# Linear-attention denominators: per-feature products moved to VectorE, one mask matmul per chunk, and the steps around them reordered

## Chip, cores and metric

The kernel runs on one core of one Trainium2 chip. The metric is device time in microseconds, the median of several executions. The profile describes one execution; its span (first to last instruction) is about 2 us shorter than the device time. PE is TensorE (PEld its weight loads), DVE is VectorE, ACT ScalarE, POOL GpSimd. "Granted clock" is the share of full TensorE speed that the chip allowed.

## The reference, cut to what matters

```python
xn = layernorm(x)                                  # x: 1 x 2048 x 640, bf16
q, k, v = split(xn @ wqkv)                         # 32 heads of 20 features
phi = lambda t: where(t > 0, t + 1, exp(t)) + 1e-6
pq, pk = phi(q), phi(k)
kv  = einsum("bhsd,bhse->bhde", pk, v);  z = einsum("bhsd->bhd", pk)
num = einsum("bhqd,bhde->bhqe", pq, kv)
den = einsum("bhqd,bhd->bhq", pq, z)[..., None] + 1e-6     # <- the change is about this
out = x + (num / den).reshape(...) @ wo + (gelu(xn @ w1 + b1) @ w2 + b2)
```

## The kernel before

Tokens stand in 16 tiles of 128 and in 4 chunks of 512. The 640 query features lie in five column groups j of 128 partitions (4 features of each of 32 heads in a group). The stages in PE's order: transposes and the GELU layer; keys for all tiles; the key-value product; query chunk 0; z; the key-value transform; query chunk 1; the product M with the output weights; chunk 0's denominator; query chunks 2 and 3; then 16 output tiles, each of 24 matmuls for the GELU branch and 10 for attention, accumulated in PSUM. In the timelines below each engine runs its instructions in the order in which the program lists them, so that order decides what waits for what. The parts that matter:

```python
def phi(src, b, nb, dst, res_dst, extra_w):        # after each query group
    scalar: et = Exp(src)
    vector: et = min(et, 1) + 1e-6
    vector: dst = max(src, 0) + et                 # src in PSUM
...
def z_step():                                      # z_sb[p, j]: sum of phi(k)
    ...
    for j in range(DT):                            # z on the head mask, one matrix per group
        vector: ZB[:, j, :] = bmask * z_sb[:, j:j+1]
...
def den_step(c):                                   # one chunk of 512 tokens
    for j in range(5): tensor: bank += ZB[:, j, :].T @ PQ[:, j, cc]
    vector: den_sb = bank + 1e-6
    vector: rden = reciprocal(den_sb)
    for j in range(5): vector: PQ[:, j, cc] *= rden
...
q_chunk(0); z_step(); kvt_step(); q_chunk(1); m_step(); den_step(0); q_chunk(2); q_chunk(3)
for c in range(4): x_again(c)                      # DMA x again, over xnT: after its last reader
for t in range(16): xb(t)                          # gpsimd: x_res[t] += b2
for t in range(16):
    out_tile(t)                                    # ends with vector: out = PSUM + x_res[t]
    if t % 4 == 0 and t // 4 + 1 < 4: den_step(t // 4 + 1)
```

Code is shortened here: `vector:` stands for an instruction recorded on that engine.

## Time and profile before

| | before |
|---|---|
| device time | 223.33 us, median of four runs (223.21, 223.23 and 223.43 fast; 255.02 slow) |
| PE busy | 214.4 of 221.4 us (97%) |
| VectorE / GpSimd busy | 125.8 / 41.7 us |
| granted clock | 1.00 |

From the page of the kernel before: busy time of an engine, its share, its number of instructions; then the busy share in 40 slices of the span, in tenths, and the granted clock.

```profile
span 221.4 us, 3944 instructions
PE 214.4 (97%) x1603; PEld 148.6 (67%) x1612; DVE 125.8 (57%) x227; ACT 74.3 (34%) x140; POOL 41.7 (19%) x74
...
PE   7699999999999999999999999999999999999994
...
DVE  2767778500004888899078549889929414811211
...
POOL 2246554200000000000000000079993000000000
PEclk9999999999999999999999999999999999999999
```

PE is the limit: every slice but the ramp (the start-up) and the last is full. VectorE has room, and GpSimd's second busy stretch (slices 27 to 31) is the 16 bias additions.

From the chain of waits of the kernel before (start us, duration us, engine, tile, line), around chunk 0's denominator; L504 is its matmuls, L507, L509 and L511 its eviction, reciprocal and multiplies, L548 the output tiles.

```profile
129.19 1.04 PE ps L504 x4
...
130.26 0.70 DVE den_sb L507
...
130.98 3.36 DVE rden L509
...
134.37 1.77 DVE PQ L511 x5
...
141.27 4.78 PE ps L548 x34
```

Two things are to be read here. Five denominator matmuls take 1.08 us where a group is recorded whole (0.215 us each; here one record is missing). And the normalization takes VectorE 5.88 us (130.26 to 136.14) while PE works on query chunks 2 and 3: the chain passes through VectorE, but PE loses only 0.26 us, just before 141.27.

From the timeline of the kernel before (start, duration, engine, line, operation, count): the multiplies of chunk 0, those of chunk 1, a residual addition between, and GpSimd's additions.

```profile
134.37 1.77 DVE L511 TENSOR_TENSOR PQ<-PQ,rden 128x512 bf16<-128x512 bf16 x5
...
146.85 0.82 DVE L554 TENSOR_TENSOR out_sb<-ps,xnT 128x640 bf16<-128x640 f32 x1 [0.74 <-POOL xnT L520]
...
151.69 6.88 DVE L511 TENSOR_TENSOR PQ<-PQ,rden 128x512 bf16<-128x512 bf16 x5
...
145.35 22.60 POOL L520 TENSOR_TENSOR xnT<-xnT,b2bc 128x640 bf16<-128x640 bf16 x16 [102.12 <-DMA xnT<-in_A_x_dram]
```

The same five multiplies take 1.77 us alone and 6.88 us beside GpSimd. Chunk 1's columns are ready at 158.57 us and first needed in tile 4, whose attention part starts at 164.08 us.

### The profile page before, as it was taken

To read this page: it belongs to the slowest core of one execution; us is meant where nothing else is said; L and a number is where in the kernel's file an instruction comes from. 1 tells how busy PE (TensorE), PEld (TensorE's weight loads), DVE (VectorE), ACT (ScalarE), POOL (GpSimd) and SP (SyncE) were. 2 spreads that over 40 slices of the span, in tenths; PEclk is the share of its full clock that TensorE was granted. 3 is DMA by queue.
4 is the path that set the end of the run, shared out by engine and by line. 5 is a ranking of instruction groups with operands and counts; after the bars stand their busy time and mean duration, and the time that the engine had idled before them with its cause. 6 is when DMAs were issued, how large, how long until landed. Compare 5 with 4: busy or idle time off the path is not lost.

```text
span 221.4 us, 3944 instructions
## 1 busy us (share of the span) xinstructions
PE 214.4 (97%) x1603; PEld 148.6 (67%) x1612; DVE 125.8 (57%) x227; ACT 74.3 (34%) x140; POOL 41.7 (19%) x74
## 2 busy tenths in 40 slices
PE   7699999999999999999999999999999999999994
PEld 2489999544447777777665865567767776777773
DVE  2767778500004888899078549889929414811211
ACT  2378877566667555111254542600000000000000
POOL 2246554200000000000000000079993000000000
PEclk9999999999999999999999999999999999999999
DMA  5999960000000000000000000254520010010011
GB/s 156 340 363 364 362 233 0 1 3 0 0 0 0 3 0 3 0 0 3 0 0 1 3 0 0 66 173 119 170 70 30 30 60 32 0 62 30 30 46 47
DMA packets 13706, 15.50 MB, mean 70 GB/s; under 512 B 632, under 2 KB 13688, under 8 KB 13688
## 3 DMA queue, kind: packets, MB, share of 16 engines
q1 hardware_dynamic: 13688, 15.24, 21.1%
q8 instruction: 13, 0.21, 0.4%
q14 instruction: 5, 0.04, 0.1%
HBM read 12.62 MB, written 2.62 MB: 69 GB/s over the span
## 4 chain that ended last, share of the span: by engine, by line
PE 88%; DVE 5%; DMA 3%; SPq 1%; issue 1%; DVEq 0%
PE ps L548 33%; PE ps L350 23%; PE ps L438 10%; PE ps L427 10%; PE ps L460 5%; PE ps L494 3%; DMA xPK<-in_A_x_dram 3%; PE ps L504 2%; PE ps L334 2%; DVE PQ L417 2%; DVE rden L509 2%; DVE PQ L511 1%; SPq L235 1%; PE ps L480 1%; SPq L231 1%
## 5 line engine op out<-in xcount | busy, mean ns | idle before, releaser
L350 PE MATMUL ps<-xnT,W 128*128 128x128 bf16 (+2 forms) x447 | 54.8, 279 | 2.1 <-DVE xnT L342 1.9
L548 PE MATMUL ps<-W,HG 128*128 128x320 bf16 x384 | 54.9, 299 | 0.3 <-DVE PQ L417 0.3
L548 PEld LDWEIGHTS ps<-W,HG 128*128 128x128 bf16 x384 | 37.5, 98 | 15.7 <-issue 0.7
L350 PEld LDWEIGHTS ps<-xnT,W 128*128 128x128 bf16 x450 | 36.1, 98 | 17.1 <-DVE xnT L342 1.5
L354 ACT ACTIVATE HG<-ps,b1c 128x128 bf16<-128x128 f32 (+2 forms) x90 | 41.1, 489 | 18.9 <-PE ps L350 17.5
L520 POOL TENSOR_TENSOR xnT<-xnT,b2bc 128x640 bf16<-128x640 bf16 x16 | 22.6, 1448 | 102.1 <-DMA xnT<-in_A_x_dram 102.1
L554 DVE TENSOR_TENSOR out_sb<-ps,xnT 128x640 bf16<-128x640 f32 x15 | 12.3, 823 | 33.4 <-PE ps L548 31.6
L414 ACT ACTIVATE ek<-ps 128x512 bf16<-128x512 f32 (+1 forms) x36 | 23.2, 645 | 23.8 <-PE ps L427 9.2
L415 DVE TENSOR_SCALAR ek<-ek 128x512 bf16<-128x512 bf16 (+1 forms) x36 | 10.9, 304 | 30.7 <-ACT ek L414 29.5
L548 PE MATMUL ps<-Msb,PQ 128*128 128x320 bf16 x160 | 24.5, 299 | 0.0
L427 PE MATMUL ps<-Wqkv,xnT 128*128 128x320 bf16 x160 | 21.9, 299 | 0.0
L438 PE MATMUL ps<-xPK,xn_tm 128*128 128x320 bf16 x160 | 21.9, 299 | 0.0
L460 PE MATMUL ps<-xnT,Wqkv 128*128 128x512 bf16 x97 | 21.6, 379 | 0.2
L427 PEld LDWEIGHTS ps<-Wqkv,xnT 128*128 128x128 bf16 x160 | 15.7, 98 | 6.2
L548 PEld LDWEIGHTS ps<-Msb,PQ 128*128 128x128 bf16 x160 | 15.7, 98 | 6.1
L438 PEld LDWEIGHTS ps<-xPK,xn_tm 128*128 128x128 bf16 x160 | 15.7, 98 | 6.1
L460 PEld LDWEIGHTS ps<-xnT,Wqkv 128*128 128x128 bf16 x100 | 11.7, 117 | 9.5
L307 DVE BATCH_NORM_STATS2 stats<-xPK 128x6 f32<-128x320 bf16 x32 | 15.1, 471 | 4.4 <-DMA xPK<-in_A_x_dram 4.4
L417 DVE SCALAR_TENSOR_TENSOR PQ<-ps,ek 128x512 bf16<-128x512 f32 x20 | 13.8, 692 | 2.1
L417 DVE SCALAR_TENSOR_TENSOR xPK<-ps,ek 128x640 bf16<-128x640 f32 x16 | 13.2, 825 | 1.7
L509 DVE RECIPROCAL rden<-den_sb 128x512 bf16<-128x512 f32 x4 | 13.4, 3353 | 0.1
L511 DVE TENSOR_TENSOR PQ<-PQ,rden 128x512 bf16<-128x512 bf16 x20 | 12.2, 674 | 0.1
(50 smaller groups left out, 113.6 us busy)
## 6 DMA issues: line engine op xcount, KB each, us to landing
xnT<-in_A_x_dram SPq DMA_DIRECT2D x4, 640.0 KB, 4.4
Wqkv<-in_A_wqkv_dram SPq DMA_DIRECT2D x3, 800.0 KB, 12.0
out_dram<-out_sb SPq DMA_DIRECT2D x15, 160.0 KB, 1.8
W<-in_B_w_dram SPq DMA_DIRECT2D x4, 480.0 KB, 5.7
xPK<-in_A_x_dram SPq DMA_DIRECT2D x3, 640.0 KB, 8.6
W<-in_B_w_dram SPq DMA_DIRECT2D x1, 1920.0 KB, 14.2
Wo<-in_A_wo_dram SPq DMA_DIRECT2D x1, 800.0 KB, 10.7
xPK<-in_A_x_dram SPq DMA_DIRECT2D x4, 160.0 KB, 4.8
```

The costliest lines, as they stand in the source:

```text
L307: Pl.ins(v, lambda e: e.bn_stats(stats[:, s, 6 * h:6 * h + 6], x_in[:, t, h * HW:(h + 1) * HW]), reads=[r_x[t]], writes=[r_stats[s]])
L350: Pl.ins("tensor", [(lambda e, k=k: e.matmul(bank(b, 0, w), W1[:, k, jb * P:(jb + 1) * P], xnT[:, k, tok], start=(k == 0), stop=(k == DT - ...
L354: Pl.ins("scalar", lambda e: e.activation(HG[:, jb, tok], bank(b, 0, w), ACT.Gelu_apprx_tanh, bias=b1c[:, jb:jb + 1]), reads=[B_[b], r_b1c ...
L414: Pl.ins("scalar", lambda e: e.activation(e2, src, ACT.Exp), reads=br, writes=[r_ek[s]])
L417: Pl.ins(v, lambda e: e.scalar_tensor_tensor(out=d2, in0=src, scalar=0.0, in1=e2, op0=ALU.max, op1=ALU.add), reads=br + [r_ek[s]], writes= ...
L427: fns.append(lambda e, k=k, h=h, b=b, t=t: e.matmul(bank(b + h, 0, HW), xnT[:, k, t * P:(t + 1) * P], Wqkv[:, k, D + h * HW:D + (h + 1) * ...
L438: Pl.ins("tensor", [(lambda e, t=t, h=h, b=b, f=f: e.matmul(bank(b + h, 0, HW), xn_tm[:, t, f * P:(f + 1) * P], PK[:, t, h * HW:(h + 1) * ...
L460: Pl.ins("tensor", [(lambda e, k=k, j=j, b=b: e.matmul(bank(b), Wqkv[:, k, j:D:DT], xnT[:, k, cc], start=(k == 0), stop=(k == DT - 1))) fo ...
L509: Pl.ins(v, lambda e: e.reciprocal(rden[:], den_sb[:]), reads=[r_den], writes=[r_rden])
L511: Pl.ins(v, lambda e, j=j: e.tensor_tensor(out=PQ[:, j, cc], in0=PQ[:, j, cc], in1=rden[:], op=ALU.mult), reads=[r_rden, r_PQ[c][j]], writ ...
L520: Pl.ins(g, lambda e: e.tensor_tensor(out=x_res[:, t, :], in0=x_res[:, t, :], in1=b2bc[:], op=ALU.add), reads=[r_xr[t // CH], r_b2], write ...
L548: return lambda e: e.matmul(bank(b + h, 0, HW), seq[i][0], seq[i][1][:, h * HW:(h + 1) * HW], start=(i == 0), stop=(i == n - 1))
```

## The change

The intent is to take work off the limiting engine. The sum over the 20 features of a head is a sum over five groups and over four partitions. The old kernel does both in five matmuls. The new one multiplies each group by z and sums the groups on VectorE, and one matmul with the plain head mask sums the partitions. To get the products done ahead of time, the diff also moves steps. Its core, with cuts marked:

```diff
+        q_chunk(0)                       # right after the keys
+        q_chunk(1)
         ... key-value product ...
-            for j in range(DT):          # in z_step
-                Pl.ins(v, lambda e, j=j: e.tensor_scalar(ZB[:, j, :], bmask[:], z_sb[:, j:j + 1], None, ALU.mult), ...)
...
         def den_step(c):
+            Pl.ins(v, lambda e: e.tensor_scalar(den_sb[:], PQ[:, 0, cc], z_sb[:, 0:1], None, ALU.mult), ...)
+            for j in range(1, DT):
+                last = j == DT - 1
+                Pl.ins(v, lambda e, j=j, last=last: e.scalar_tensor_tensor(
+                    out=sden[:] if last else den_sb[:], in0=PQ[:, j, cc], scalar=z_sb[:, j:j + 1],
+                    in1=den_sb[:], op0=ALU.mult, op1=ALU.add), ...)
+
+        def den_step2(c):
-            Pl.ins("tensor", [(lambda e, j=j: e.matmul(bank(b), ZB[:, j, :], PQ[:, j, cc], ...)) for j in range(DT)], ...)
+            Pl.ins("tensor", lambda e: e.matmul(bank(b), bmask[:], sden[:], start=True, stop=True), ...)
             ... eviction, reciprocal, five multiplies as before ...
...
-        q_chunk(0)
         z_step()
         kvt_step()
-        q_chunk(1)
+        q_chunk(2)
+        den_step(0)
         m_step()
-        den_step(0)
-        q_chunk(2)
         q_chunk(3)
+        den_step2(0)
...
         for t in range(NT):
-            out_tile(t)
             if t % CH == 0 and t // CH + 1 < NC:
                 den_step(t // CH + 1)
+            out_tile(t)
+            if t % CH == 1 and t // CH + 1 < NC:
+                den_step2(t // CH + 1)
```

More of the change, by code (lines that the diff above doesn't have):

```diff
@@ L165, in bass_parallel_sum__linear_attn_block__dense_activation_gelu__prompt_kernel @@
         maskKV = [sb(f"maskKV{t}", [P, Wd[t]], BF16) for t in range(DT)]
-        ZB = sb("ZB", [P, DT, P], BF16)
+        sden = sb("sden", [P, CW], BF16)
         onesb = sb("onesb", [P, 1], BF16)
@@ L221, in bass_parallel_sum__linear_attn_block__dense_activation_gelu__prompt_kernel @@
         r_M = [R_("M%d" % j) for j in range(DT)]
-        r_zsum, r_zhl, r_z, r_ZB = R_("zsum"), R_("zhl"), R_("z"), R_("ZB")
+        r_zsum, r_zhl, r_z, r_sden = R_("zsum"), R_("zhl"), R_("z"), R_("sden")
         r_den, r_rden = R_("den"), R_("rden")
@@ L431, in bass_parallel_sum__linear_attn_block__dense_activation_gelu__prompt_kernel, with q_chunk @@
             phi(pair(b), b, 2, PK[:, t, :], r_PK[t], [r_x[t]])
+        def q_chunk(c):
+            cc = slice(c * CW, (c + 1) * CW)
+            for j in range(DT):
+                b = take(1)
+                Pl.ins("tensor", [(lambda e, k=k, j=j, b=b: e.matmul(
+                    bank(b), Wqkv[:, k, j:D:DT], xnT[:, k, cc],
+                    start=(k == 0), stop=(k == DT - 1))) for k in range(DT)],
+                    reads=[r_Wq] + r_xnT[c * CH:(c + 1) * CH], writes=[B_[b]])
+                phi(bank(b), b, 1, PQ[:, j, cc], r_PQ[c][j], [])
+        q_chunk(0)
+        q_chunk(1)
         Pl.ins(v, lambda e: e.memset(KVT, 0.0), writes=[r_KVT] + r_W1)
@@ L453, in bass_parallel_sum__linear_attn_block__dense_activation_gelu__prompt_kernel @@
                reads=[r_zsum, r_zhl], writes=[r_zhl])
-        def q_chunk(c):
-            cc = slice(c * CW, (c + 1) * CW)
-            for j in range(DT):
-                b = take(1)
-                Pl.ins("tensor", [(lambda e, k=k, j=j, b=b: e.matmul(
-                    bank(b), Wqkv[:, k, j:D:DT], xnT[:, k, cc],
-                    start=(k == 0), stop=(k == DT - 1))) for k in range(DT)],
-                    reads=[r_Wq] + r_xnT[c * CH:(c + 1) * CH], writes=[B_[b]])
-                phi(bank(b), b, 1, PQ[:, j, cc], r_PQ[c][j], [])
         def z_step():
@@ L472, in z_step @@
             Pl.ins(v, lambda e: e.tensor_copy(z_sb[:], bank(b, 0, DT)), reads=[B_[b]], writes=[r_z])
-            for j in range(DT):
-                Pl.ins(v, lambda e, j=j: e.tensor_scalar(ZB[:, j, :], bmask[:], z_sb[:, j:j + 1], None, ALU.mult),
-                       reads=[r_z, r_bmask], writes=[r_ZB])
         def kvt_step():
@@ L502, in den_step @@
             cc = slice(c * CW, (c + 1) * CW)
+            Pl.ins(v, lambda e: e.tensor_scalar(den_sb[:], PQ[:, 0, cc], z_sb[:, 0:1], None, ALU.mult),
+                   reads=[r_z, r_PQ[c][0]], writes=[r_den])
+            for j in range(1, DT):
+                last = j == DT - 1
+                Pl.ins(v, lambda e, j=j, last=last: e.scalar_tensor_tensor(
+                    out=sden[:] if last else den_sb[:], in0=PQ[:, j, cc], scalar=z_sb[:, j:j + 1],
+                    in1=den_sb[:], op0=ALU.mult, op1=ALU.add),
+                    reads=[r_z, r_PQ[c][j], r_den], writes=[r_sden if last else r_den])
+        def den_step2(c):
+            cc = slice(c * CW, (c + 1) * CW)
             b = take(1)
-            Pl.ins("tensor", [(lambda e, j=j: e.matmul(bank(b), ZB[:, j, :], PQ[:, j, cc],
-                                                       start=(j == 0), stop=(j == DT - 1))) for j in range(DT)],
-                   reads=[r_ZB] + r_PQ[c], writes=[B_[b]])
+            Pl.ins("tensor", lambda e: e.matmul(bank(b), bmask[:], sden[:], start=True, stop=True),
+                   reads=[r_bmask, r_sden], writes=[B_[b]])
             Pl.ins(v, lambda e: e.tensor_single_scalar(den_sb[:], bank(b), 1e-6, ALU.add),
```

## The prediction

> **What bounds the kernel now.** TensorE. The page's first part has PE busy 97% of a 221.4 us span, and the chain of waits is 88% PE, 5% VectorE. The granted clock is at full speed in every slice. VectorE is busy 57%, GpSimd 19%. In the timeline the only PE gap after the ramp is 0.26 us before the first output tile (141.27 us).
>
> **Removed.** Four of five denominator matmuls per chunk, four chunks: 16. The chain shows such a group of five as 1.08 us, so 0.215 us each: 3.4 us of PE work, on the chain. Five small mask multiplies (1.4 us of VectorE) go too, off the chain.
>
> **Added.** Per chunk one tensor_scalar and four scalar_tensor_tensor of 128x512 on VectorE. The trace has 690 ns for the eviction form and 692 ns for the existing scalar_tensor_tensor of that width; estimate 3.4 us a chunk, 13.7 us in all. VectorE has room in total, so the question is where the work stands.
>
> **Moved.**
> 1. Query chunks 0 and 1 go ahead of the key-value product. The matmul that needs its last eviction (ACT, 0.70 us) is then covered only by the z matmuls (0.36 us): estimate 0.45 us PE wait. The old 0.26 us gap goes.
> 2. Chunk 0's normalization (denominator eviction 0.69, reciprocal 3.35, five multiplies 1.77 us, uncontended) stood between the M product and query chunks 2 and 3, with two chunks of PE work to hide it. Now it follows the last query chunk. Let T be the end of that chunk on PE (estimate 140.4 us). The last phi ends at T+1.7, the reciprocal at T+5.8. Output tile 0 needs the normalized columns at T+3.5 (24 matmuls, 3.26 us, after the one mask matmul).
> 3. The reload of x is still released at T, so GpSimd starts its 16 bias additions at about T+4.3, as before (141.0 to 145.35). In the trace before, the one set of multiplies that overlaps them took 6.88 us rather than 1.77: each slipped in after one GpSimd addition (period 1.54 us). The Trainium skill, "SBUF — State Buffer", "Who interferes with whom", says that a VectorE instruction with two SBUF inputs contends with a GpSimd instruction reading SBUF; this trace agrees, and the additions to out_sb, with one PSUM input, stay at 0.82 us. Now the multiplies that tile 0 waits for, and next the new scalar_tensor_tensors of chunk 1, fall in that window.
>
> Estimate: first multiply done at T+7.3, fifth at T+13.5; tile 0 ends at T+13.9 instead of T+4.8: 9.1 us lost. Chunk 1's products then run at 1.5 to 1.8 us each until T+22.2; tile 1 ends at T+18.5, so the mask matmul of chunk 1 waits 3.8 us. Later chunks are clear of GpSimd and hide.
>
> **Sum.** 223.4 - 3.4 + 0.45 - 0.26 + 9.1 + 3.8 = 233.1; I say 232.5 us, range 226.5 to 236.5. Chances: faster by over 2% 0.05, within 2% 0.10, slower by over 2% 0.85.
>
> **What would show it.** Denominator matmuls: 20 to 4. PE waits in the first output tile, named after the multiplies, 8 to 10 us in all; one PE wait of 2 to 5 us before the mask matmul of chunk 1, on the last scalar_tensor_tensor. The multiplies' mean for chunk 0 near 1.5 us, other chunks 0.35. New products 0.7 us without GpSimd, 1.5 to 1.8 beside it. A wait of half a microsecond before the key-value transform. Little else on PE.
>
> **What would make it wrong.** If the contention gives way (several VectorE instructions per GpSimd one), tile 0 loses only about 3 us and the result is near 223 to 225. If several microseconds of PE idleness lower the granted clock, the time is 2 to 3 us longer. If query chunks and phi interleave worse on VectorE, T moves.

## The result

The changed kernel takes 232.86 us median (four runs, 232.46 to 234.79) against 223.33 us: slower, by a ratio of 1.0446 with a 95% interval of 1.0373 to 1.0519. A ratio here is the mean time of one kernel's fast runs over that of the other's fast runs of the same rounds, so it is not quite the ratio of the medians. Executions over 1.5% slower than the fastest of the same kernel are left out of the means.

From the page of the changed kernel, the lines that answer to those of before:

```profile
span 230.9 us, 3930 instructions
PE 214.2 (93%) x1587; PEld 147.3 (64%) x1596; DVE 145.8 (63%) x242; ACT 74.3 (32%) x140; POOL 43.7 (19%) x74
...
PE   7699999999999999999999998258799999999995
...
DVE  3767786400019888999906939999987578391211
...
POOL 2245653100000000000000000999930000000000
PEclk9999999999999999999999999758999999999999
```

There are 16 PE instructions fewer (1603 to 1587). PE is now idle in slices 25 to 29, beside GpSimd's additions, and the granted clock dips there. PE's total of 214.2 us has not fallen, mainly because some matmuls ran at half clock: tile 1's 24 GELU matmuls alone took 1.8 us more, as the next lines show.

From the timeline of the changed kernel, PE: L516 is the mask matmul, L558 the output tiles (HG the GELU part, PQ the attention part that needs normalized columns).

```profile
140.09 0.38 PE L516 MATMUL ps<-sden,bmask 128*128 128x512 bf16 x1
140.31 3.42 PE L558 MATMUL ps<-W,HG 128*128 128x320 bf16 x24
147.71 0.71 PE L558 MATMUL ps<-Msb,PQ 128*128 128x320 bf16 x2 [3.98 <-DVE PQ L522]
149.24 0.71 PE L558 MATMUL ps<-Msb,PQ 128*128 128x320 bf16 x2 [0.81 <-DVE PQ L522]
...
153.84 0.71 PE L558 MATMUL ps<-Msb,PQ 128*128 128x320 bf16 x2 [0.82 <-DVE PQ L522]
154.35 5.20 PE L558 MATMUL ps<-W,HG 128*128 128x320 bf16 x24
...
162.80 3.42 PE L558 MATMUL ps<-W,HG 128*128 128x320 bf16 x24 [1.90 <-DVE sden L508]
```

Output tile 0 gets its normalized columns one group at a time, 1.53 us apart. Tile 1 then takes 5.2 us for the part that takes 3.42 us elsewhere, and tile 2 waits for chunk 1's products (the mask matmul before it has no record of its own here).

From the timeline of the changed kernel, VectorE and GpSimd: L520 reciprocal, L522 multiplies, L504 and L508 products of chunk 1.

```profile
142.64 3.35 DVE L520 RECIPROCAL rden<-den_sb 128x512 bf16<-128x512 f32 x1
146.03 7.75 DVE L522 TENSOR_TENSOR PQ<-PQ,rden 128x512 bf16<-128x512 bf16 x5
153.71 1.61 DVE L504 TENSOR_SCALAR den_sb<-PQ,z_sb 128x512 f32<-128x512 bf16 x1
155.35 5.37 DVE L508 SCALAR_TENSOR_TENSOR den_sb<-PQ,z_sb,den_sb 128x512 f32<-128x512 bf16 x3
160.76 1.76 DVE L508 SCALAR_TENSOR_TENSOR sden<-PQ,z_sb,den_sb 128x512 bf16<-128x512 bf16 x1
...
173.49 2.33 DVE L508 SCALAR_TENSOR_TENSOR den_sb<-PQ,z_sb,den_sb 128x512 f32<-128x512 bf16 x3
...
144.63 24.55 POOL L531 TENSOR_TENSOR xnT<-xnT,b2bc 128x640 bf16<-128x640 bf16 x16 [101.75 <-DMA xnT<-in_A_x_dram]
```

Beside GpSimd a multiply takes about 1.5 us, the first product (L504) 1.61 us and the others 1.8 us. Free of it (chunk 2, at 173.49) three products take 2.33 us, 0.78 each. VectorE runs without a gap from 141.9 to past 162 us: for those 20 us it is the limit.

The balance, from these timelines: 16 matmuls less -3.4; a wait before the key-value transform +0.5; the old gap gone -0.3; tile 0 ends at 154.3 instead of 145.1 (which would be 4.8 us after the last query chunk at 140.25) +9.3; tile 1 and the wait after it, 8.45 us from 154.35 to 162.80 instead of 4.6, +3.8; and PE enters the query stage 0.3 us earlier (87.6 against 87.9). The sum is +9.6 us; the spans differ by 9.5 us.

### The profile page after: what moved, and what is told of

Its sections match the earlier page's. It is cut to its first block, busy times and chain, and to the rows that moved or that the text cites. A ratio compares the mean times of both kernels' runs of the same rounds, so it can differ in the third digit from the quotient of the medians.

```text
span 230.9 us, 3930 instructions
## 1 busy us (share of the span) xinstructions
PE 214.2 (93%) x1587; PEld 147.3 (64%) x1596; DVE 145.8 (63%) x242; ACT 74.3 (32%) x140; POOL 43.7 (19%) x74
## 4 chain that ended last, share of the span: by engine, by line
PE 82%; DVE 11%; DMA 3%; SPq 1%; issue 1%; ACT 0%; DVEq 0%
PE ps L558 28%; PE ps L350 22%; PE ps L452 9%; PE ps L427 9%; PE ps L438 8%; DVE PQ L522 3%; PE ps L495 3%; DMA xPK<-in_A_x_dram 3%; DVE den_sb L508 2%; PE ps L334 2%; DVE PQ L417 1%; DVE rden L520 1%; DVE sden L508 1%; PE ps L481 1%; SPq L235 1%
## 5 line engine op out<-in xcount | busy, mean ns | idle before, releaser
L558 PE MATMUL ps<-W,HG 128*128 128x320 bf16 x384 | 56.7, 305 | 2.0 <-DVE sden L508 1.9
L558 PEld LDWEIGHTS ps<-W,HG 128*128 128x128 bf16 x384 | 38.4, 100 | 16.1
L531 POOL TENSOR_TENSOR xnT<-xnT,b2bc 128x640 bf16<-128x640 bf16 x16 | 24.6, 1571 | 101.7 <-DMA xnT<-in_A_x_dram 101.7
L558 PE MATMUL ps<-Msb,PQ 128*128 128x320 bf16 x160 | 26.6, 309 | 7.3 <-DVE PQ L522 7.3
L558 PEld LDWEIGHTS ps<-Msb,PQ 128*128 128x128 bf16 x160 | 15.3, 98 | 15.6 <-DVE PQ L522 9.9
L522 DVE TENSOR_TENSOR PQ<-PQ,rden 128x512 bf16<-128x512 bf16 x20 | 14.1, 768 | 0.1
L520 DVE RECIPROCAL rden<-den_sb 128x512 bf16<-128x512 f32 x4 | 13.4, 3353 | 0.1
```

Of the source, the lines that this page charges most:

```text
L520: Pl.ins(v, lambda e: e.reciprocal(rden[:], den_sb[:]), reads=[r_den], writes=[r_rden])
L522: Pl.ins(v, lambda e, j=j: e.tensor_tensor(out=PQ[:, j, cc], in0=PQ[:, j, cc], in1=rden[:], op=ALU.mult), reads=[r_rden, r_PQ[c][j]], writ ...
L531: Pl.ins(g, lambda e: e.tensor_tensor(out=x_res[:, t, :], in0=x_res[:, t, :], in1=b2bc[:], op=ALU.add), reads=[r_xr[t // CH], r_b2], write ...
L558: return lambda e: e.matmul(bank(b + h, 0, HW), seq[i][0], seq[i][1][:, h * HW:(h + 1) * HW], start=(i == 0), stop=(i == n - 1))
```

## Experiments

Three theories could explain a loss of this shape. **A**: it comes from the order, that is chunk 0's normalization now stands behind the last query chunk, and VectorE instructions with two SBUF inputs alternate there with GpSimd's additions. **B**: PE's idle time lowered its clock, and that is the loss. **C**: the products are simply too much work for VectorE. All kernels below gave correct results. The experiments ran in three sets, each on another chip and each beside the kernel before: e1 to e4; e1b, e5, e6 and e7; e8 to e10. The ratios compare within a set; differences between experiments of different sets, or from the changed kernel, are of medians.

### 1. GpSimd's additions held back (e1_hold_bias)

```diff
-        for t in range(NT):
-            xb(t)
...
             if t % CH == 0 and t // CH + 1 < NC:
                 den_step(t // CH + 1)
+            if t == 0:
+                Pl.wait_event(g, r_sden.w)   # chunk 1's products done
+                for u in range(NT):
+                    xb(u)
```

> The changed kernel, but GpSimd's 16 bias additions are held back until chunk 1's products are done. Theory A (the loss is chunk 0's normalization standing behind the last query chunk, stretched by VectorE instructions with two SBUF inputs alternating with GpSimd additions): the five multiplies fall from 1.55 us to 0.35 us each, the products from 1.8 to 0.75 us, tile 0 still loses about 3 us, the wait before chunk 1's mask matmul goes; 223 us. Theory B (the idle PE dropped its clock and that is the loss): only what the shorter wait brings back of the clock, at most 2 us: 231. Theory C (the products themselves overload VectorE): nothing changes, 233.

Measured: 229.48 to 230.61 us in three fast runs, ratio 1.0296 (1.0269 to 1.0323). The expected 223 us was missed by 7 us.

### 2. The same kernel again (e1b_hold_again)

> The first experiment once more, for a profile in the fast state: it took 229.5 to 230.6 us where 223 was expected. Theory A, mended: holding the GpSimd additions until chunk 1's products are done moves them over chunk 2's products, which then run at 1.8 us each, and PE waits about 5 us before chunk 2's mask matmul; the five multiplies of chunk 0 take 1.77 us and PE waits about 2.7 us in tile 0. If instead PE waits longer in tile 0 or has no wait in chunk 2, theory A is wrong about where the time goes.

Measured: 229.97 us, one run (state unknown, but its time and clock, 0.985, are those of the fast runs above). From its timeline, PE, VectorE and GpSimd:

```profile
147.27 2.85 PE L556 MATMUL ps<-Msb,PQ 128*128 128x320 bf16 x10 [2.79 <-DVE PQ L522]
...
154.84 0.38 PE L516 MATMUL ps<-sden,bmask 128*128 128x512 bf16 x1
...
176.91 0.39 PE L516 MATMUL ps<-sden,bmask 128*128 128x512 bf16 x1 [3.22 <-DVE sden L508]
177.14 5.10 PE L556 MATMUL ps<-W,HG 128*128 128x320 bf16 x24
...
146.79 1.77 DVE L522 TENSOR_TENSOR PQ<-PQ,rden 128x512 bf16<-128x512 bf16 x5
...
169.69 5.37 DVE L508 SCALAR_TENSOR_TENSOR den_sb<-PQ,z_sb,den_sb 128x512 f32<-128x512 bf16 x3
...
152.18 24.13 POOL L531 TENSOR_TENSOR xnT<-xnT,b2bc 128x640 bf16<-128x640 bf16 x16 [108.54 <-DVE sden L508]
```

With GpSimd away, the five multiplies of chunk 0 are back at 1.77 us, tile 0 waits 2.8 us in all instead of 7.3, and chunk 1's mask matmul waits for nothing. But the additions now lie over chunk 2's products, which slow to 1.79 us each; its mask matmul waits 3.2 us (about 5 were expected), and the GELU part of the tile after it runs 1.7 us slow. The collision was moved, not removed. My first expectation had looked only at chunk 1.

### 3. GpSimd's additions in two lots (e7_hold_twice)

The cut shows the edit against experiment 1.

```diff
-            if t == 0:
-                Pl.wait_event(g, r_sden.w)
-                for u in range(NT):
+            if t in (0, CH):
+                Pl.wait_event(g, r_sden.w)   # chunk 1's, then chunk 2's products done
+                for u in range(2 * t, 2 * t + 2 * CH):
                     xb(u)
```

> The changed kernel with GpSimd's additions in two lots: those of tiles 0 to 7 held until chunk 1's products are done, those of tiles 8 to 15 until chunk 2's are done. Mended theory A: no products beside GpSimd, so no wait before any mask matmul; what stays is the bare tail of about 2.7 us in tile 0, perhaps with a clock drop of up to 1.7 us behind it: 222.5 to 225 us. If the clock alone were the loss, about as the first experiment, 230 us.

Measured: 223.85 us median of four runs, one of them slow (226.32, at a clock of 0.983); fast runs of 222.91, 223.13 and 224.58; ratio 0.9978 (0.9881 to 1.0075), as fast as before. PE's waits in its profile, in total us, times, longest:

```profile
PE ps L556 <- DVE PQ L522: 2.8, 1, 2.8
```

Only the bare tail of tile 0 is left (beside waits of the ramp and the 0.5 us before the transform), and the loss is gone. Holding the additions back changes no arithmetic and no amount of work, so about 9 us of the changed kernel's time was the collision with GpSimd, with what followed from it.

### 4. Chunk 0 normalized before the last query chunk (e2_norm_early)

```diff
         m_step()
-        q_chunk(3)
         den_step2(0)
+        q_chunk(3)
```

> The changed kernel, but chunk 0's mask matmul, reciprocal and multiplies go before query chunk 3 instead of after it; the arithmetic is the same. Theory A: tile 0 no longer waits for multiplies; chunk 1's products now begin when the delayed phis of chunk 3 end, beside GpSimd, and last 8.7 us, so the mask matmul of chunk 1 waits about 5 us; 225 us. Theory C: the same sum of VectorE work, so no gain, 233 us.

Measured: 227.60 us, ratio 1.0190 (1.0169 to 1.0211), which leaves the 2% verdict against the kernel before unclear. From its timeline, PE at tile 2:

```profile
155.84 4.97 PE L558 MATMUL ps<-W,HG 128*128 128x320 bf16 x24 [5.83 <-DVE sden L508]
```

One moved line brings 5 us. The wait in tile 0 is gone, as expected. The wait for chunk 1's products is 5.8 us rather than 5, and the tile behind it ran 1.5 us slow, which I had not counted; these two make 2.3 of the 2.6 us by which 225 was missed.

### 5. The new order with the old five matmuls (e3_order_only)

The products are taken out, ZB and its five matmuls are back (in `den_step2`, at its new places).

> The changed kernel's order with the old arithmetic: five matmuls with the masked z per chunk, no products on VectorE. Theory A: tile 0 waits for its multiplies as in the changed kernel (9 us lost), no wait before chunk 1's denominator, the clock drop behind the wait now costs its 1.9 us in the open, and PE works 3.4 us more: about 234 us, as slow as the changed kernel. Theory C: the products are gone, so about 223.5 us.

Measured: 234.48 us, ratio 1.0506 (1.0479 to 1.0532). Theory C falls: without a single product on VectorE the new order is as slow as the whole change. From its timeline, tile 1 on PE:

```profile
154.66 6.03 PE L550 MATMUL ps<-W,HG 128*128 128x320 bf16 x24
```

### 6. A chunk's multiplies as one instruction (e4_one_multiply)

```diff
-            for j in range(DT):
-                Pl.ins(v, lambda e, j=j: e.tensor_tensor(out=PQ[:, j, cc], in0=PQ[:, j, cc], in1=rden[:], op=ALU.mult), ...)
+            Pl.ins(v, lambda e: e.tensor_tensor(out=PQ[:, :, cc], in0=PQ[:, :, cc],
+                                                in1=rden[:].unsqueeze(1).to_broadcast([P, DT, CW]), op=ALU.mult), ...)
```

> The changed kernel with a chunk's five normalizing multiplies as one instruction over 5x512 columns. Theory A with the cost per instruction (each waits for one GpSimd addition): one wait of at most 1.4 us and 1.4 us of work, so tile 0's columns are ready at about 8.5 us after the last query chunk instead of 13.5, chunk 1's products end 5 us earlier too; 228 us. Rival (GpSimd and VectorE share bandwidth, so the same elements take the same time): the one multiply takes 7 to 8 us, and tile 0 waits longer for its first column; 233 to 235 us.

Measured: 228.29 us, ratio 1.0212 (1.0186 to 1.0238), again unclear by the 2% rule, but 4.6 us below the changed kernel. From its timeline, VectorE:

```profile
146.33 2.63 DVE L521 TENSOR_TENSOR PQ<-PQ,rden 128x2560 bf16<-128x2560 bf16 x1
```

The same 2560 columns that took 7.75 us in five instructions take 2.63 us in one, beside the same additions; alone the one instruction takes 1.49 us. If the two engines shared a bandwidth, the one instruction would have taken 7 to 8 us. So the cost here is one wait per instruction.

### 7 and 8. PE kept busy in the waits of tile 0 (e5_filler, e6_order_filler)

```diff
                 for i in range(n):
+                    if t == 0 and i >= JT:       # before each attention group of tile 0
+                        fb = (b + 6) % 8         # a free bank
+                        Pl.ins("tensor", [lambda e: e.matmul(bank(fb), warm[:, 0:P], warm[:], start=True, stop=True)
+                                          for _ in range(17 if i == JT else 3)], reads=[r_warm], writes=[B_[fb]])
                     Pl.ins("tensor", [mm(i, 0), mm(i, 1)], ...)
```

First in the changed kernel:

> The changed kernel with dummy matmuls on PE in the waits of output tile 0 (17 before the first normalized column group, 3 before each of the other four), so that PE stays busy and keeps its clock. Theory A: chunk 1's products on VectorE end at the same time, so tile 1 gets about 2 us faster and the wait before chunk 1's mask matmul grows from 1.9 to about 4 us; time unchanged, 232.5 to 233.3 us. Theory B (clock): 2 us or more faster, 231 or below.

Then in the kernel of experiment 5, where no VectorE work waits behind tile 1:

> The same dummy matmuls in the kernel that has the changed order with the old five matmuls, where nothing waits behind tile 1: here the clock drop should lie in the open. Tile 1 took 7.4 us there instead of 4.6, so about 2.7 us faster than that kernel: 231.8 us. If the dummies are no cure for the clock, or the slow tile 1 had another cause, no change: 234.5 us.

Measured: 234.26 us (233.19 to 235.36), ratio 1.0447, in the changed kernel; 231.82 us, ratio 1.0355, in the other, against 234.48 us without the dummies. From the timeline of e5_filler, PE at tiles 1 and 2, and last the GELU part of tile 1 in e6_order_filler, to be set against the 6.03 us of experiment 5:

```profile
154.11 3.42 PE L558 MATMUL ps<-W,HG 128*128 128x320 bf16 x24
157.37 1.52 PE L558 MATMUL ps<-Msb,PQ 128*128 128x320 bf16 x10
162.56 0.61 PE L516 MATMUL ps<-sden,bmask 128*128 128x512 bf16 x1 [3.67 <-DVE sden L508]
162.96 5.88 PE L558 MATMUL ps<-W,HG 128*128 128x320 bf16 x24
...
154.44 3.42 PE L550 MATMUL ps<-W,HG 128*128 128x320 bf16 x24
```

The dummies kept the clock: tile 1 is back at full speed in both kernels. In the changed kernel this only lengthened the next wait from 1.9 to 3.7 us, because VectorE finishes the products at 162.5 us either way; and that longer wait now slowed tile 2, which I had not expected. The median is 1.4 us above the changed kernel's and above the 232.5 to 233.3 expected; the ratio to the runs of before in the same rounds (some of which took 225 us at a clock of 0.992) is the same. The run of this kernel whose mean clock was 1.00 took 233.19 us, no better than the changed kernel at 0.977. So theory B does not explain the loss, though the clock drop is real: in the other kernel, where nothing hides it, the same dummies won 2.7 us by the medians, as expected (the two were run in different sets; by the ratios, 1.0506 and 1.0355, it is 3.4 us).

### 9 and 10. The new arithmetic in the old order (e8_all, e9_all_five_mult)

```diff
-        q_chunk(0)                      # after the keys
-        q_chunk(1)
...
+        q_chunk(0)
         z_step()
         kvt_step()
-        q_chunk(2)
-        den_step(0)
-        m_step()
-        q_chunk(3)
-        den_step2(0)
+        q_chunk(1)
+        den_step(0)                     # products: VectorE is idle during the M product
+        m_step()
+        den_step2(0)
+        q_chunk(2)
+        q_chunk(3)
```

With GpSimd's two lots (experiment 3) and, in e8_all, the one multiply (experiment 6).

> The new arithmetic in the old order: query chunk 0, z, key-value transform, query chunk 1, chunk 0's products (VectorE idles during the M product), M product, chunk 0's normalization, query chunks 2 and 3; GpSimd's additions in two lots as before, and the five multiplies of a chunk as one instruction. Theory A: no PE wait over 0.3 us after the ramp, so the 16 removed matmuls show: 223.4 - 3.4 - 0.3 = 219.7 us. If the products cost PE something that order can't hide, 222 us or more.

> As the one before, but with five multiplies per chunk. Theory A: the multiplies of chunk 1 are done at about 163 us, about when tile 4 asks for them, so the same within 0.5 us: 219.7 to 220.5 us.

Measured: e8_all 219.77 us (219.41 to 221.16), ratio 0.9852 (0.9819 to 0.9886); e9_all_five_mult 219.73 us, ratio 0.9858 (0.9819 to 0.9896). The intervals exclude 1. PE's waits in the profile of e8_all, all of them:

```profile
PE ps L350 <- DVE xnT L342: 1.5, 1, 1.5
PE ps L294 <- DVE warm L262: 1.2, 1, 1.2
PE ps L334 <- DVE xn_tm L327: 0.6, 1, 0.6
PE ps L556 <- DVE PQ L417: 0.2, 1, 0.2
```

The first three belong to the ramp; after it PE waits 0.2 us. The removed matmuls now show: PE is busy for 211.2 us instead of 214.4, its waits sum to 3.5 us as against 3.6 in the kernel before, and the span is 3.3 us shorter (218.1 against 221.4). GpSimd's two lots are no likely source of that gain, since PE waited for nothing but 0.26 us after the ramp in the kernel before; they were not run there alone. The one multiply adds nothing here, since in this order five are in time too.

### 11. Control: the kernel before with one multiply (e10_before_one)

> The kernel before with only the multiplies of a chunk made one instruction, as a control: its multiplies are off the chain of waits, so 223.2 to 223.5 us. If it is as fast as the two others, their gain does not come from the removed matmuls.

Measured: 222.86 us, ratio 1.0001 (0.9959 to 1.0043). So the gain of the two kernels above is not the one multiply's.

## Why the prediction was right

The time (232.5 predicted, 232.86 measured) and the verdict were right, and so was most of the mechanism. That the number is so close is partly luck: the terms sum to 233.1, and why 232.5 was named instead isn't said.

- **What bounds the kernel, and what the matmuls are worth.** Right. The 16 matmuls were put at 3.4 us; with all new waits taken away (e8_all) the kernel is 3.5 us faster than before, against an expectation of 3.4 plus 0.3.
- **Tile 0.** Predicted: first multiply done 7.3 us after the last query chunk, fifth at 13.5, 9.1 us lost. In the trace the first columns are used at 7.5 us (147.71 - 140.25), the multiplies end at 13.5 us (153.78 - 140.25), and 9.3 us are lost: the tile ends 14.1 us after the last query chunk instead of the 4.8 that its matmuls need.
- **The contention.** Predicted from 6.88 against 1.77 us in the trace before; shown by experiments 2 and 3 (without overlap 1.77 us) and 6 (one wait per instruction). The page "SBUF — State Buffer", section "Who interferes with whom", of the Trainium skill names the ground, a port pair that VectorE and GpSimd share under an exclusive lock. The traces agree in what they can show; they don't show the port.
- **Chunk 1's products.** Predicted at 1.5 to 1.8 us each; measured 1.61 for the first and 1.79 for the others. The first is no case of the two SBUF inputs that the prediction names: it reads one tensor and a column of z, and still goes from 0.48 to 1.61 us (1.50 in e1b_hold_again), while the reciprocal, with one input too, stays at 3.35 us beside the additions. The loss of 3.8 us was right as a sum but not in its parts: half is the wait (1.9 us), half is tile 1 at a lowered clock (1.8 us). With tile 1 at full speed, in e5_filler, the wait alone is 3.7 us, as predicted.
- **The clock.** The prediction named it as a risk that would add 2 to 3 us. It happened, and no run shows that it added time, for VectorE was later than PE anyway (experiment 7). The windows view of the changed kernel has it. A line gives the stretch, its length, the busy times of PE, PEld, DVE, ACT and POOL with instruction counts, and then the granted clock (after it DMA share and GB/s):

```profile
147.70:154.30 6.60, 3.31 (x10) 0.80 (x11) 6.60 (x5) 0.00 (x0) 6.60 (x5) 0.50 0.44 122
154.30:162.80 8.50, 6.61 (x35) 4.09 (x35) 8.36 (x6) 0.00 (x0) 8.50 (x6) 0.78 0.23 76
```

  The clock is 1.00 up to the end of the 4.0 us wait, 0.50 from 147.7 us on, while tile 0 gets its columns one group at a time, and comes back within tile 1. The page "TensorE: Matmul & The Clock Gate", section "What's actually happening", says that the clock falls to half after an idle window of about 3.4 us; here a wait of 4.0 us came before it (the last section has shorter ones).
- **Smaller misses.** PE's waits in tile 0 sum to 7.3 us, not 8 to 10, because each pair of matmuls itself took longer at half clock (0.71 us, against 0.45 in e5_filler). A product alone takes 0.48 us (tensor_scalar) and 0.78 us, not 0.69 for both. Chunk 1's multiplies still met the last GpSimd additions (2.80 us for five), which cost nothing. The wait before the transform was 0.52 us against 0.45.

## What to carry to other kernels

Moving work off the limiting engine pays only if the engine that takes it is free at that place: read in the timeline, step by step, what the receiving engine does between the producer and the first consumer, and don't put a long serial tail (here eviction, reciprocal and multiplies) behind the last work that could hide it. Here VectorE instructions with two SBUF inputs, and the one-input first product too, paid one wait each beside a stream of GpSimd instructions, so keep the two apart in time, or merge the many into one. And when a fix moves a collision, look for the next place that it lands on.

## What the Trainium skill lacked or had wrong

- "SBUF — State Buffer", "Who interferes with whom": the rule agrees with every run, but it doesn't say what a stream of instructions on both engines does. Here they alternate one for one: a bf16 multiply of 128x512 goes from 0.35 to about 1.54 us and a scalar_tensor_tensor from 0.78 to 1.79 us, while a GpSimd addition goes from 1.40 to 1.57 us beside a multiply and to 1.84 us beside a product. The advice that follows, one multiply of 2560 columns (2.63 us) rather than five of 512 (7.75 us), no page gives for this collision.
- "VectorE: DVE Perf Modes", the perf-mode tier table has no row for scalar_tensor_tensor. With a bf16 and an fp32 input in SBUF, 512 columns took 0.78 us each in a row.
- "TensorE: Matmul & The Clock Gate", "What's actually happening": the window of about 3.4 us of idleness is no safe threshold. The same wait of 2.8 us in tile 0 left the granted clock at 1.00 in e7_hold_twice's profile and halved it in e1b_hold_again, where it was 0.50 in the 3 us after the wait; in e2_norm_early it fell 2.15 us into the wait of 5.83 us. The page calls the window free-running; that might make the moment differ from run to run, but it doesn't say why less than a whole idle window was enough, and no run here shows the window.
